# Another order of calls in an attention and feed-forward kernel on one core

## The chip, the core and the metric

The kernel runs on one core of a Trainium2 chip. The metric is the device time of one execution in microseconds (us). Before the change it is 411.36 us (median of 3 runs, 410.83 to 411.58).

## The reference

Attention with normalized q and k, followed by a feed-forward layer with a parametric ReLU, all in float32:

```python
# q, k, v: 8 x 12 x 448 x 64; w_in: 768 x 2048; w_out: 2048 x 768; alpha: 2048
def rmsnorm(x, g):
    return x / np.sqrt(np.mean(x * x, axis=-1, keepdims=True) + 1e-06) * g
scores = (1 / np.sqrt(64)) * rmsnorm(q, g_q) @ rmsnorm(k, g_k).transpose(0, 1, 3, 2)
attn = np.exp(scores - scores.max(-1, keepdims=True))
attn = attn / (attn.sum(-1, keepdims=True) + 1e-09)
x = (attn @ v).transpose(0, 2, 1, 3).reshape(3584, 768)
h = x @ w_in
out = (np.maximum(h, 0) + alpha * np.minimum(h, 0)) @ w_out
```

## The kernel before

The 96 heads (8 batches of 12) are worked in 24 groups of four heads, three groups to a batch. The order of all work is one text, PLAN: a list of some 1,300 calls such as `score(2,5,0)`, which a loop at the end of the kernel carries out one after the other. Each call issues its instructions to a fixed engine, and each engine works through its own instructions strictly in that order, waiting on semaphores for what the others must have done. So the order of PLAN decides what queues behind what on TensorE (PE), VectorE (DVE), ScalarE (ACT), GpSimd (POOL) and on the two queues that issue transfers, SyncE's (SP) and POOL's own.

For one group y the calls are these.

- `load_qk(y)` (SP) loads q and k as `nat`. The memory of q and k is taken over from an earlier group, so the transfer waits until that group's `scale` has been done.
- `square(y,nm)` (POOL for nearly all groups), `reduce(y,nm)` (DVE, sums of squares), `root(y)` (ACT, two small instructions for the inverse root), `scale(y,nm)` (DVE up to group 3, POOL from group 4 on) normalize q and k to float16.
- `turn(y)` or `turn_one(y,nm)` transposes them by matmuls on PE and copies them back by DVE, up to group 8; from group 9 on `flip` (DVE) and `weigh` (ACT) do this.
- `score(y,j,spare)` makes a block of scores on PE, seven to a group, in one of two PSUM tiles `sc` or, with spare, in a third, `acc`. `soft(y,j)` takes their exponential on ACT.
- `den` and `attend` sum the exponentials and multiply them with v on PE; `log` and `invert` (ACT) make the reciprocal of the sums; `times` (DVE) multiplies and writes the attention's result `xT`. A batch's first two groups go together (`0+1`), its third alone (`2`).

For one batch b, `up(b,ft)` multiplies `xT` with a block of 128 columns of w_in on PE (16 blocks). `slope` multiplies the result by alpha, `larger` (DVE) takes the larger of the two and writes `gT`. For batch 0, `begin(ft)` does the part of the first four blocks that needs groups 0 and 1 alone. `down` and, later, the `qa`, `qb`, `qc` and `quad` calls multiply `gT` with w_out; `mix_weights`, `mix_two` and `mix_rest` (POOL, mostly) make the sums that these use.

The first group has calls of its own, in parts by heads and columns (`part_square`, `part_reduce`, `part_root`, `part_scale`, `part_turn`, `part_copy`). `opening()` issues the transfers of groups 0, 1 and 2 and of the gains and alphas, then some matmuls on zeros (`spin`), and a transpose `ct` of gains and alphas, which `gains()` copies to where they are used; k's copies out of PSUM are multiplied by that gain. Further `spin` calls put matmuls on zeros, whose result nobody uses, between others. `follow(y,nm)` has POOL copy one element of what DVE's `scale` wrote: it makes POOL wait there for DVE. `load_w_in(c)`, `load_w_out(c)` and `load_v(b)` issue the transfers of weights and v from POOL's queue.

Of the kernel before, what the change touches and what calls it, by code (L numbers as in the profile page):

```python
# [43 lines left out]
up(0,1,0) begin(2) begin(3) root(4) up(0,2,0) up(0,3,1) up(0,4,0) scale(4,q) slope(0,0) soft(3,1)  # L44
larger(0,0) score(3,2,0) score(3,6,0) slope(0,1) load_qk(7) follow(2,k) larger(0,1) slope(0,4)
slope(0,2) slope(0,3) larger(0,4) up(0,5,0) larger(0,2) larger(0,3) root(5) soft(3,6) slope(0,5)
soft(3,2) larger(0,5) up(0,6,0) scale(4,k) turn(4) scale(5,q) up(0,8,0) score(4,0,0) slope(0,6)
score(4,1,1) square(6,k) larger(0,6) slope(0,8) score(3,5,0) up(0,9,0) load_w_out(1) scale(5,k)
soft(4,0) square(7,q) larger(0,8) up(0,11,0) load_qk(8) score(4,2,0) score(3,3,0) soft(3,5)
load_v(1) square(7,k) up(0,7,1) soft(4,1) slope(0,9) up(0,10,0) reduce(6,q) square(8,q) reduce(6,k)  # L50
load_w_out(2) soft(4,2) up(0,12,0) slope(0,11) larger(0,9) soft(3,3) score(3,4,0) slope(0,10)
score(4,3,0) larger(0,11) larger(0,10) slope(0,7) larger(0,7) up(0,13,0) soft(3,4) slope(0,12)
larger(0,12) turn(5) up(0,14,0) square(8,k) soft(4,3) score(4,6,0) slope(0,13) score(4,4,1) root(6)
slope(0,14) larger(0,13) up(0,15,0) scale(6,q) reduce(8,q) soft(4,4) score(5,4,0) larger(0,14)
scale(6,k) score(5,0,1) reduce(7,q) slope(0,15) larger(0,15) down(1,0,0) score(5,2,1) score(4,5,0)
soft(4,6) soft(5,0) soft(5,4) soft(5,2) score(5,1,0) soft(4,5) down(0,0,0) turn(6) load_w_out(3)
den(3+4,1) reduce(7,k) attend(3+4,0,0) score(5,5,0) score(5,6,0) soft(5,1) mix_weights(0,1) log(3+4)
invert(3+4) soft(5,5) soft(5,6) mix_weights(0,3) attend(3+4,1,0) score(6,0,1) score(5,3,0) soft(6,0)
score(6,4,0) down_end(0,0) down(2,0,0) soft(5,3) root(7) scale(7,q) load_qk(9) soft(6,4) scale(7,k)
den(5,0) attend(5,0,1) down_end(1,0) mix_weights(0,2) times(3+4,0,0) times(3+4,1,0) times(3+4,1,1)  # L60
load_qk(10) log(5) down(0,1,0) reduce(8,k) invert(5) down_end(2,0) times(5,0,1) times(5,0,0)
times(5,0,3) times(5,0,2) score(6,5,1) mix_weights(0,0) score(6,1,0) down_end(0,1) score(6,6,0)
soft(6,5) turn(7) up(1,1,1) square(9,q) down(1,1,0) root(8) reduce(9,q) soft(6,6) score(6,3,1)
score(7,0,0) slope(1,1) score(6,2,0) up(1,2,0) up(1,0,0) soft(6,1) soft(7,0) soft(6,3) square(9,k)
up(1,3,1) up(1,4,0) slope(1,2) slope(1,0) larger(1,1) down_end(1,1) reduce(9,k) root(9) larger(1,2)
# [1032 lines left out]
```

## Time and profile before

| | |
|---|---|
| median of 3 runs | 411.36 us (410.83 to 411.58) |
| the profiled execution | 410.69 us, with a span of 408.6 us from its first to its last instruction |
| PE busy | 395.3 us, 97% of the span |
| DVE, ACT, POOL busy | 268.3, 270.4 and 299.9 us |
| granted TensorE clock | 1.000 |
| DMA | 58.39 MB, 143 GB/s on average |

In the profile, `PE hT L726 <- DVE xT L709` reads: PE, about to write the tile hT by an instruction of line 726, waited for DVE's writing of xT by line 709. In the rows of the timeline the columns are the start in us, the duration in us from the first to the last of the instructions put together, the engine, the line, the operation, what is written and read, the shapes, and the number of instructions; in brackets stands the idle time before, with what ended it. PEld are PE's loads of weights, which overlap its matmuls. In the rows of busy time by stretches the columns are the stretch, its length, the busy us with the number of instructions for PE, PEld, DVE, ACT and POOL, the granted clock, the share of the DMA engines and GB/s.

### The profile page before, as it was taken

Reading aid. Unit: us, or ns where it says so; the run is one execution under the profiler, and the core shown is the slowest. Engines: PE = TensorE matmul, PEld = TensorE weight load, DVE = VectorE, ACT = ScalarE, POOL = GpSimd, SP = SyncE. Lnnn points to the kernel's source line nnn. Section 1 sums busy time; section 2 is a strip of 40 time slices with the busy share of each in tenths; the row PEclk is TensorE's granted clock in tenths of the full one; section 3 lists DMA queues with packets and bytes.
Section 4 is the critical chain, followed back from the end, with each engine's and each line's share of the span. In section 5 each row is a group of like instructions: output and inputs, shape, how many; then the busy total and the mean of one; then the engine's idle time right before and its main releaser. Section 6 shows DMA issues by size and latency. Waiting matters only on the chain.

```text
span 408.6 us, 11992 instructions
## 1 busy us (share of the span) xinstructions
PE 395.3 (97%) x5083; PEld 210.3 (51%) x5083; DVE 268.3 (66%) x480; ACT 270.4 (66%) x405; POOL 299.9 (73%) x200
## 2 busy tenths in 40 slices
PE   7688999999999999999999999999999999999996
PEld 3344445555455445554455455555555455655664
DVE  3957874676766685779678678886668545654422
ACT  5597686757885876767886987686876874245110
POOL 7977998497796998997796995589496809600780
PEclk9999999999999999999999999999999999999999
DMA  7999699796776794579952595794516000230143
GB/s 260 242 280 227 110 265 165 173 239 177 125 180 154 173 203 108 119 172 185 232 130 83 136 240 145 147 217 102 140 38 131 21 2 22 59 79 0 39 98 98
DMA packets 37222, 58.39 MB, mean 143 GB/s; under 512 B 4769, under 2 KB 28977, under 8 KB 37169
## 3 DMA queue, kind: packets, MB, share of 16 engines
q1 hardware_dynamic: 23232, 45.43, 43.2%
q0 software_dynamic: 13536, 11.81, 19.1%
q8 instruction: 39, 0.64, 0.7%
q10 hardware_dynamic: 400, 0.39, 0.3%
q14 instruction: 15, 0.11, 0.1%
HBM read 58.40 MB, written 11.01 MB: 170 GB/s over the span
## 4 chain that ended last, share of the span: by engine, by line
PE 88%; DVE 4%; DMA 3%; POOL 3%; issue 1%; POOLq 0%; DVEq 0%
PE hT L726 25%; PE hTa L726 9%; PE sc L588 8%; PE op L792 7%; PE qx L854 5%; PE av L613 5%; PE qz L854 4%; PE qc L854 4%; PE oq L854 4%; PE qxa L854 3%; PE avb L613 2%; PE dn L613 2%; PE oqm L854 2%; DMA w_in_sb<-in_moe_w_in_dram 2%; POOL nat L376 2%; DMA arena<-in_g_k_dram 2%
## 5 line engine op out<-in xcount | busy, mean ns | idle before, releaser
L602 ACT ACTIVATE expT<-sc 128x896 f16<-128x896 f32 x168 | 146.3, 916 | 40.9 <-PE sc L588 39.2
L726 PE MATMUL hT<-xT,w_in_sb 128*128 128x448 f16 x558 | 115.9, 353 | 1.6 <-DVE xT L709 1.4
L726 PEld LDWEIGHTS <-w_in_sb 128*128 128x128 f16 x768 | 73.0, 98 | 74.5 <-issue 9.9
L423 POOL TENSOR_TENSOR qs<-nat,rr 128x896 f16<-128x896 f32 x30 | 65.7, 2221 | 26.5 <-ACT rr L417 23.4
L766 ACT ACTIVATE gT<-hT,cols 128x448 f16<-128x448 f32 x92 | 58.4, 636 | 40.0 <-PE hT L726 38.9
L772 DVE TENSOR_TENSOR gT<-hT,gT 128x448 f16<-128x448 f32 x93 | 57.3, 619 | 38.2 <-ACT gT L766 37.5
L365 POOL TENSOR_TENSOR nat<-nat 128x896 f32<-128x896 f32 x30 | 50.7, 1697 | 8.1 <-DMA nat<-in_q_dram 7.7
L588 PE MATMUL sc<-qT,kT 64*32 64x448 f16 (+1 forms) x1092 | 49.4, 355 | 4.3 <-ACT expT L602 1.7
L854 PEld LDWEIGHTS <-gT 128*128 128x128 f16 x352 | 33.4, 98 | 25.5 <-issue 4.1
L726 PE MATMUL hTa<-xT,w_in_sb 128*128 128x448 f16 x198 | 42.9, 353 | 0.0
L842 POOL TENSOR_TENSOR gs<-gT 128x1024 f16<-128x1024 f16 x4 | 8.5, 2127 | 36.7 <-DVE gT L772 36.7
L709 DVE TENSOR_TENSOR xT<-av,rden 64x448 f16<-64x448 f32 (+1 forms) x37 | 27.2, 736 | 10.7 <-ACT rden L671 4.6
L386 DVE TENSOR_REDUCE sp<-nat 128x28 f32<-128x896 f32 x30 | 32.1, 1070 | 2.1 <-POOL nat L365 2.0
L588 PEld LDWEIGHTS <-kT 64*32 64x32 f16 (+1 forms) x1092 | 16.7, 93 | 32.4 <-issue 23.0
L792 PE MATMUL op<-w_out_sb,gT 128*128 128x384 f16 x176 | 30.3, 326 | 0.2 <-DVE xT L709 0.2
L766 ACT ACTIVATE gT<-hTa,cols 128x448 f16<-128x448 f32 x33 | 21.0, 636 | 10.5 <-PE hTa L726 10.0
L772 DVE TENSOR_TENSOR gT<-hTa,gT 128x448 f16<-128x448 f32 x33 | 20.4, 618 | 10.6 <-ACT gT L766 10.2
L613 PEld LDWEIGHTS <-vt 64*32 64x32 f16 x1344 | 19.7, 92 | 12.2 <-issue 1.9
L792 PEld LDWEIGHTS <-gT 128*128 128x128 f16 x192 | 18.3, 98 | 14.5 <-issue 3.0
L613 PE MATMUL av<-expT,vt 64*32 64x448 f16 x896 | 24.3, 350 | 0.0
L850 POOL TENSOR_TENSOR gT<-gT 128x1024 f16<-128x1024 f16 x11 | 23.5, 2133 | 0.0
L854 PEld LDWEIGHTS <-arena 128*128 128x128 f16 x136 | 12.6, 98 | 10.5 <-issue 2.3
(151 smaller groups left out, 572.5 us busy)
## 6 DMA issues: line engine op xcount, KB each, us to landing
nat<-in_q_dram SPq DMA_DIRECT2D x60, 216.0 KB, 4.1
nat<-in_k_dram SPq DMA_DIRECT2D x60, 216.0 KB, 5.0
out_dram<-osb SPq DMA_DIRECT2D x107, 96.0 KB, 3.1
vt<-in_v_dram POOLq DMA_DIRECT2D x8, 672.0 KB, 7.8
w_in_sb<-in_moe_w_in_dram POOLq DMA_DIRECT2D x24, 128.0 KB, 7.3
w_out_sb<-in_moe_w_out_dram POOLq DMA_DIRECT2D x4, 768.0 KB, 8.6
nat<-in_k_dram SPq DMA_DIRECT2D x6, 448.0 KB, 7.8
nat<-in_q_dram SPq DMA_DIRECT2D x5, 448.0 KB, 6.7
```

What stands on the lines that cost most here:

```text
L365: nc.gpsimd.tensor_mul(out=sqs[y, nm], in0=t[:, :, :HD], in1=t[:, :, :HD])
L386: nc.vector.tensor_reduce(out=parts[y][:, ts("qk".index(nm), 4 * J), :1], in_=sqs[y, nm], axis=AXIS_X, op=ALU.add,)
L423: nc.gpsimd.tensor_mul(out=t.rearrange("p j d n -> p n j d"), in0=nat[y, nm][:, :, :HD].rearrange("p (n j) d -> p n j d", j=J), in1=r.unsq ...
L588: nc.tensor.matmul(out=sc[ds(64 * g + m * c, m), par, :S].rearrange("p (j c) -> p j c", j=J), lhsT=kT[ds(64 * par, 64), j, g, ts(c, m)], r ...
L602: nc.scalar.activation(out=expT[y][:, j], in_=scs[y, j][:, :, :S], func=AF.Exp, scale=QK_SCALE, bias=EXP_BIAS,)
L613: nc.tensor.matmul(out=accs[g][ds(32 * n, 32), :S], lhsT=weights(g, y, par, c, j), rhs=expT[y][ds(64 * g, 64), j, par, :], start=(j == 0), ...
L709: nc.vector.tensor_mul(out=o, in0=p, in1=q)
L726: nc.tensor.matmul(out=hT[:, :S], lhsT=w_in_sb[:, block_of(g, i), ts(ft, 128)], rhs=xT[b][:, g, i, :], start=(i == 0 and g == 0), stop=(i ...
L766: nc.scalar.activation(out=g, in_=hT[:, :S], func=AF.Copy, scale=alpha_sb[:, ft : ft + 1])
L772: nc.vector.tensor_max(out=g, in0=hT[:, :S], in1=g)
L792: nc.tensor.matmul(out=op[:, :OH], lhsT=gT[:, ft, ts(tile % J, 128)], rhs=w_out_sb[:, ft, ts(oh, OH)], start=(ft == 0), stop=(ft == NF - 1),)
L854: nc.tensor.matmul(out=bank[:, c], lhsT=g[:, ft], rhs=v[:, ft, c], start=(first and ft == 0), stop=(ft == HF - 1), skip_group_check=True,)
```

## The change

PLAN has another order. From the start to the first `up` nearly every engine's order differs, further on the order is similar but differs in many places. In the opening: the `spin` matmuls of `opening()` come down to one call `spin(17,0)`, and of the later ones `spin(2,0)` stays; the transpose of gains and alphas is a call of its own, `factors()`, behind q's transposes; the two first reductions of q change places; `square(1,k)` goes from POOL to ACT, the copies of q and of the first part of k from DVE to ACT; `square(3,k)` comes ahead of `square(3,q)`, in two halves; w_in is loaded in halves (`load_w_in(c,lo,hi)`), spread between the squares; three of the four `follow` calls are gone, and the last comes some 220 calls later. Over the whole PLAN 25 `slope` calls are marked for DVE, where 3 were; `score`, `den`, `attend` and `up` use the third PSUM tile in other places. A `slope` and a `square` are now told their engine in PLAN, and `soft`, `begin` and `up` can be called in any order of their blocks.

The diff, with PLAN up to the first `up` of batch 0:

```diff
 PLAN = """
-opening() part_square(q,0:1,0:7,act) part_square(q,1:2,0:7,act) part_reduce(q,0:1,0:7) spin(2,0)
-part_reduce(q,1:2,0:7) part_root(q,0:7) part_square(k,0:2,0:3,act) part_scale(q,0:7,7,pool)
-part_reduce(k,0:2,0:3) part_square(k,0:2,3:7,act) square(1,q) load_w_in(1) spin(1)
-part_reduce(k,0:2,3:7) part_root(k,3:7) reduce(1,q) square(1,k) part_root(k,0:3) gains()
-part_turn(q,r0-7) load_qk(3) spin(1,0) part_scale(k,0:3,3,vec) part_turn(k,r0-3)
-part_scale(k,3:7,4,vec) part_copy(q,0:7,vec) part_turn(k,r3-7) load_v(0) reduce(1,k) follow(0,k)
-square(2,q) part_copy(k,0:3,vec) part_copy(k,3:7,vec) root(1) square(2,k) score(0,0,0) soft(0,0)
-reduce(2,q,0) score(0,4,1) load_w_in(0) score(0,3,0) spin(1) reduce(2,q,1) soft(0,3) score(0,1,0)
-scale(1,k) scale(1,q) soft(0,4) score(0,2,0) soft(0,2) reduce(2,k) score(0,6,1) turn_one(1,q)
-soft(0,1) turn_one(1,k) score(1,0,1) score(1,3,0) spin(1) score(1,2,0) soft(0,6) root(2) soft(1,0)
-load_qk(4) soft(1,3) scale(2,k) scale(2,q) follow(2,q) square(3,q) square(3,k) load_w_in(2)
-soft(1,2) score(0,5,1) score(1,1,0) soft(0,5) soft(1,1) score(1,5,0) turn(2) soft(1,5) score(1,6,1)
-soft(1,6) reduce(3,q,None) score(1,4,0) score(2,0,0) soft(1,4) den(0+1,0) follow(1,k) soft(2,0)
-log(0+1) load_qk(5) score(2,1,0) spin(1) reduce(3,k,0+1) attend(0+1,1,0) score(2,6,0) score(2,4,1)
-attend(0+1,0,1) soft(2,1) root(3) score(2,3,1) invert(0+1) scale(3,q) scale(3,k) score(2,2,0)
-load_w_in(3) soft(2,4) soft(2,6) times(0+1,1,0) times(0+1,1,1) square(4,q) times(0+1,0,0) turn(3)
-score(2,5,0) square(4,k) load_qk(6) reduce(4,q,None) soft(2,3) soft(2,2) soft(2,5) den(2,0) log(2)
-reduce(4,k,None) invert(2) attend(2,0,1) score(3,0,1) square(5,q) square(5,k) times(2,0,0)
-score(3,1,0) begin(0) reduce(5,q) square(6,q) soft(3,0) begin(1) up(0,0,0) load_w_out(0) reduce(5,k)
...
+opening() part_square(q,0:1,0:7,act) part_square(q,1:2,0:7,act) part_reduce(q,1:2,0:7)
+part_reduce(q,0:1,0:7) spin(17,0) part_root(q,0:7) part_scale(q,0:7,7,pool)
+part_square(k,0:2,0:3,act) part_reduce(k,0:2,0:3) part_square(k,0:2,3:7,act) load_w_in(1,0,4)
+part_root(k,0:3) load_v(0) part_turn(q,r0-7) part_reduce(k,0:2,3:7) factors()
+part_scale(k,0:3,3,vec) part_root(k,3:7) gains() part_scale(k,3:7,4,vec) part_turn(k,r0-3)
+square(1,k,act) square(2,q,pool,2) reduce(1,k) part_copy(q,0:7,act) square(1,q,act)
+part_copy(k,0:3,act) part_turn(k,r3-7) part_copy(k,3:7,vec) score(0,6,1) reduce(2,q,0) score(0,1,0)
+reduce(1,q) score(0,4,1) load_qk(3) soft(0,6) score(0,0,0) root(1) reduce(2,q,1) scale(1,q)
+scale(1,k) score(0,5,0) square(2,k) load_w_in(2,4,8) reduce(2,k) turn_one(1,q) score(0,3,0)
+soft(0,1) square(3,k,pool,2) soft(0,0) turn_one(1,k) load_qk(4) soft(0,4) soft(0,5) score(0,2,0)
+score(1,5,0) soft(0,3) root(2) score(1,6,1) score(1,0,0) scale(2,k) spin(2,0) score(1,2,1)
+scale(2,q) load_w_in(0,0,4) square(3,q) soft(0,2) reduce(3,k,0+1) score(1,1,0) square(4,q) turn(2)
+soft(1,6) soft(1,5) soft(1,0) load_w_in(0,4,8) soft(1,2) score(1,3,0) soft(1,1) score(1,4,1)
+reduce(3,q,None) soft(1,3) soft(1,4) den(0+1,1) load_w_in(2,0,4) score(2,0,1) root(3)
+attend(0+1,0,1) reduce(4,q,None) score(2,3,0) log(0+1) score(2,4,1) soft(2,0) attend(0+1,1,0)
+score(2,1,1) invert(0+1) load_qk(5) soft(2,4) soft(2,3) square(4,k) load_qk(6) score(2,5,0)
+score(2,2,0) soft(2,1) soft(2,5) scale(3,q) score(2,6,1) scale(3,k) square(5,q) soft(2,2)
+square(5,k) times(0+1,0,0) times(0+1,1,0) soft(2,6) times(0+1,1,1) load_qk(7) turn(3)
+reduce(4,k,None) den(2,1) log(2) load_w_in(3,0,4) attend(2,0,1) reduce(5,q) root(4) invert(2)
+begin(3) scale(4,q) times(2,0,0) begin(1) begin(2) up(0,1,0) load_w_out(1) up(0,2,0) begin(0)
+up(0,0,0) reduce(5,k) score(3,1,0) slope(0,1) scale(4,k) root(5) score(3,0,0) square(6,k)
...
-    def load_w_in(c):
+    def load_w_in(c, lo, hi):
...
+        for m in range(lo, hi):
+            e, n = divmod(m % 4, 2)
...
+            if m < 4:
+                src = moe_w_in[:512].rearrange("(n x p) f -> n p x f", n=4, p=32)
...
+            else:
+                src = moe_w_in[512:].rearrange("(n g e p) f -> e n p g f", n=2, g=2, e=2)
...
-    def square(y, nm):
+    def square(y, nm, eng=None, n=1):
...
+            if eng is nc.scalar:
+                nc.scalar.activation(out=sqf[:, c], in_=src[:, c], func=AF.Square)
...
-        if nm == "k":
+        if nm == "k" and eng is nc.scalar:
+            nc.scalar.activation(out=o, in_=tp, func=AF.Copy, scale=gain[:, 0:1])
+        elif nm == "k":
...
     def soft(y, j):
-        if j == 0:
+        if y not in expT:
...
-        elif ft == 2:
+        elif ft not in begun:
...
                 up_part(begun[n], 0, n, G - 1, G)
+                raised[0, n] = begun[n], gT[:, n, :S]
...
-    def slope(b, ft):
+    def slope(b, ft, eng=None):
         hT, g = raised[b, ft]
-        if b == 0 and ft in (2, 3, NF - 4):
+        if eng is nc.vector:
...
         load_qk(1, True)
         load_qk(2)
 
-        spin(2)
-        spin(17, False)
+    def factors():
         ct = psf.tile([128, 512], FP32, name="ct", tag="mm")
         nc.tensor.transpose(ct[:, : NF + 2], rows, ident32[: NF + 2, : NF + 2])
```

More of the change, by code (lines that the diff above doesn't have):

```diff
@@ L43 @@
-score(3,1,0) begin(0) reduce(5,q) square(6,q) soft(3,0) begin(1) up(0,0,0) load_w_out(0) reduce(5,k)
[L44 to L65, printed above, removed]
@@ new lines @@
+square(8,k) larger(0,9) reduce(8,k) larger(0,10) score(4,6,1) root(6) reduce(7,k) down(1,0,0)
+score(5,5,1) score(4,2,0) score(4,4,0) soft(4,6) square(8,q) soft(5,2) down(0,0,0) score(5,6,0)
+reduce(7,q) reduce(8,q) scale(6,k) score(5,3,0) soft(4,4) follow(0,k) scale(6,q) root(7) load_qk(9)
+soft(4,2) turn(6) down_end(0,0) scale(7,q) den(3+4,1) attend(3+4,0,1) load_qk(10) soft(5,5)
+soft(5,6) attend(3+4,1,0) down_end(1,0) soft(5,3) den(5,1) log(3+4) invert(3+4) attend(5,0,1)
+scale(7,k) score(6,0,1) log(5) score(6,4,0) times(3+4,0,0) down(2,0,0) mix_weights(0,2) down(0,1,0)
@@ new lines @@
+score(6,5,1) invert(5) times(3+4,1,0) times(3+4,1,1) times(5,0,0) times(5,0,1) load_v(2)
+times(5,0,3) down_end(2,0) square(9,q) times(5,0,2) score(6,6,0) score(6,1,0) square(9,k)
+reduce(9,q) soft(6,0) soft(6,4) root(8) down_end(0,1) turn(7) up(1,1,1) up(1,0,0) slope(1,0,vec)
+down(1,1,0) score(6,2,0) score(6,3,1) larger(1,0) mix_weights(0,1) up(1,4,0) soft(6,5) up(1,3,0)
+score(7,4,1) soft(6,6) mix_weights(0,0) score(7,0,0) load_qk(11) slope(1,1) larger(1,1) score(7,2,0)
+up(1,7,0) scale(8,q) soft(6,1) down_end(1,1) reduce(9,k) up(1,2,0) soft(6,2) soft(6,3) load_qk(12)
@@ new lines @@
+larger(1,12) reduce(10,q) up(1,13,0) score(8,0,0) square(11,q) mix_weights(1,3) score(8,3,0)
+slope(1,11) larger(1,11) soft(7,3) den(6+7,0) down(2,1,0) slope(1,14) fold(10) root(10) scale(10,k)
+flip(9,q) square(11,k) slope(1,15) flip(9,k) slope(1,13) larger(1,14) load_qk(13) score(8,1,0)
+soft(8,3) score(8,5,1) larger(1,15) score(8,4,0) larger(1,13) down(3,0,0) scale(10,q) log(6+7)
+score(8,6,0) invert(6+7) soft(8,0) soft(8,1) reduce(11,q) down_end(2,1) reduce(11,k) down_end(3,0)
+flip(10,k) soft(8,5) score(8,2,0) soft(8,4) weigh(9) attend(6+7,0,0) attend(6+7,1,0) fold(11)
@@ L1034 @@
     acts = dict(
+        factors=factors,
         attend=attend, begin=begin, den=den, den_pre=den_pre, down=down, down_end=down_end,
```

278 lines of the change are left out of this document (137 added, 141 removed).

## The prediction

> **What bounds the kernel now.** I read four views in this order: the page's shares and slices, the busy time in two stretches, TensorE's own waits, and the timeline of the first 45 us, where the change lies. The profiled execution took 410.69 us with a span of 408.6, so 2.1 lie outside the span; the median of the runs shown is 411.36, 0.67 above this execution. I sum against 410.69 and add 0.67 at the end. 0.2% of this kernel, about what a measurement can tell from no change, is 0.8 us.
>
> ```profile
> PE   7688999999999999999999999999999999999996
> 0.00:41.30 41.30, 32.55 (x470) 15.78 (x471) 27.58 (x42) 29.26 (x47) 33.69 (x53) 1.00 1.02 250
> 41.30:408.60 367.30, 362.71 (x4614) 194.50 (x4613) 240.71 (x439) 241.11 (x358) 266.25 (x148) 1.00 0.59 131
> PE hT L726 <- DVE xT L709: 0.2, 1, 0.2
> PE sc L588 <- DVE kT L569: 0.2, 1, 0.2
> PE op L792 <- DVE xT L709: 0.2, 1, 0.2
> ```
>
> The slices show TensorE (PE) full from the fifth on. From 41.3 us it is busy 362.71 of 367.30 us, and its listed waits there are three of 0.2 us; what else is missing lies behind its last matmul. So from 41.3 us the end is set by the amount of PE work. Before 41.3 PE is also marked busy for 32.55 us, but much of that is `spin` and matmuls whose successors wait. What the change can win is how early PE becomes full. These rows end the opening:
>
> ```profile
> 32.59 0.56 POOL L339 DMA_DIRECT2D w_in_sb<-in_moe_w_in_dram  x1 [1.10 <-DMA w_in_sb<-in_moe_w_in_dram]
> 34.08 1.71 POOL L339 DMA_DIRECT2D w_in_sb<-in_moe_w_in_dram  x3 [0.93 <-DMA w_in_sb<-in_moe_w_in_dram]
> 35.80 3.33 POOL L376 TENSOR_TENSOR nat<-nat 128x896 f32<-128x896 f32 x2
> 39.16 1.09 DVE L395 TENSOR_REDUCE ss<-nat 128x14 f32<-128x896 f32 x1 [0.55 <-POOL nat L376]
> 40.16 1.08 DVE L709 TENSOR_TENSOR xT<-av,rden 128x896 f16<-128x896 f32 x1
> 41.30 0.92 PE L726 MATMUL hT<-xT,w_in_sb 128*128 128x448 f16 x4 [1.23 <-DVE xT L709]
> ```
>
> Read upward: up(0,0) waits 1.23 us for xT of group 2 (times(2,0,0), VectorE, DVE). That stood behind reduce(4,k), which waited 0.55 for GpSimd's (POOL) square(4,k). POOL was late because it had issued w_in(2) and w_in(3) first, waiting 1.10 and 0.93 for earlier transfers.
>
> **The change, step by step.** I walk the new order through these rows, shifting times by what precedes each call.
>
> ```profile
> 3.92 1.15 DVE L457 TENSOR_REDUCE ss<-nat 128x7 f32<-128x448 f32 x2 [2.51 <-ACT nat L450]
> 5.65 1.69 POOL L474 TENSOR_TENSOR qs<-nat,rr 128x896 f16<-128x896 f32 x1 [1.34 <-ACT rr L469]
> 7.29 2.25 POOL L339 DMA_DIRECT2D w_in_sb<-in_moe_w_in_dram  x4
> 10.65 0.62 DVE L1030 TENSOR_TENSOR gain<-cols 128x1 f32<-128x1 f32 x1
> 11.15 0.91 POOL L329 DMA_DIRECT2D vt<-in_v_dram  x1
> 11.19 1.15 DVE L474 TENSOR_TENSOR qs<-nat,rr 128x384 f16<-128x384 f32 x2
> 12.55 3.46 POOL L376 TENSOR_TENSOR arena<-arena 128x448 f32<-128x448 f32 x3
> 12.79 1.07 DVE L395 TENSOR_REDUCE ss<-nat 128x14 f32<-128x896 f32 x1
> 13.79 0.79 DVE L495 TENSOR_SCALAR kT<-tps,gain 128x384 f16<-128x384 f16 x2
> 13.90 0.23 ACT L416 ACTIVATE rr<-ss 128x28 f32<-128x28 f32 x1 [3.94 <-DVE ss L395]
> 14.68 4.97 ACT L602 ACTIVATE expT<-sc 128x896 f16<-128x896 f32 x6 [0.30 <-PE sc L588]
> 15.55 2.41 DVE L436 TENSOR_TENSOR arena<-nat,rr 128x896 f16<-128x896 f32 x2
> 20.13 2.08 DVE L436 TENSOR_TENSOR qs<-arena,rr 128x896 f16<-128x896 f32 x2
> ```
>
> *First scores.* The two q reductions (1.15 together) swap, so the first must wait for the second square: 0.55 later for part_root(q). POOL's part_scale(q) then runs from 6.20 to 7.89, four w_in issues (2.25) to 10.1, load_v (0.91) to 11.05, and there square(2,q) starts, since follow(0,k), which held it to 12.55, is now far later. `gains` still ends at 11.27, because it waits for a transfer that no edit moves, and part_scale(k,3:7) is ready at 11.19, 0.14 us into POOL's half square (3.46 for two halves and a whole: 0.9 a half). Do they collide? The pair of scale(1) calls, of which the first began while POOL's square ran on to 16.01, took 2.41 us; the same pair for group 2, with no square beside it, took 2.08. So an overlap of 0.46 (15.55 to 16.01) cost 0.33, two thirds of it; by that share the overlap of 0.8 with the half square would cost 0.55. The bounds are nothing and 1.7 (both halves first). I take 0.8, the first half waited out to its end, because the row also fits a wait for all but the last of the square.
>
> The Trainium skill, "SBUF — State Buffer", section "Who interferes with whom", has a rule that speaks against dropping the follow() calls: a DVE tensor_tensor with both inputs in SBUF and a GpSimd op that reads SBUF share one read port, and the second to issue waits the whole other instruction out. By that rule the cost is 0.8 and by the row's share 0.55, which would make the sum 0.25 lower; the 2.41 against 2.08 agrees with it in kind.
>
> So part_scale(k,3:7) ends at 12.6, reduce(1,k) (1.07) at 13.7, the vector copy of k (half of 0.79) at 14.05, and the first exponential on ScalarE (ACT) some 0.5 later, as before (copy 13.79 to 14.2, exponential 14.68): at 14.5, only 0.2 sooner. The copy of q, the copy of k's first part and both squares of group 1 lie on ACT from about 9.4 on, where it stood idle for 3.94 us ahead of root(1) at 13.90; no row shows ACT copying transposes from PSUM; at the 0.83 of an exponential from there (4.97 for six) four such steps fill 3.3 of that stretch, and even at 1.2 each they end at 14.2, in time: I put nothing. Beyond that, each excess would go straight to the first exponential; a gain is excluded, since k waits for `gains` and not for ACT.
>
> *ACT from 14.5 on.* It has 21 exponentials, three roots, log and invert before the last exponential of group 2.
>
> ```profile
> 20.24 7.50 ACT L602 ACTIVATE expT<-sc 128x896 f16<-128x896 f32 x9 [0.23 <-PE sc L588]
> 27.77 0.92 ACT L666 ACTIVATE rden<-dn 128x896 f32<-128x896 f32 x1
> 27.96 1.02 PE L1000 MATMUL spin<-gT 128*128 128x448 f32 x2
> 35.08 0.92 ACT L602 ACTIVATE expT<-sc 128x896 f16<-128x896 f32 x1 [0.48 <-PE sc L588]
> 35.13 0.67 DVE L569 TENSOR_SCALAR kT<-tps,gain 128x896 f16<-128x896 f16 x1
> 36.74 0.92 ACT L666 ACTIVATE rden<-dn 128x896 f32<-128x896 f32 x1 [0.74 <-PE dn L613]
> 37.69 0.95 ACT L671 ACTIVATE rden<-rden 128x896 f32<-128x896 f32 x1
> 36.42 1.52 PE L613 MATMUL av<-expT,vt 64*32 64x448 f16 x56
> 37.87 0.57 PE L588 MATMUL sc<-qT,kT 64*64 64x448 f16 x8
> 38.37 1.69 PE L726 MATMUL hT<-xT,w_in_sb 128*128 128x448 f16 x8
> ```
>
> Nine exponentials in 7.50 are 0.83 each: 17.5 for 21. A root is two instructions of 0.23 (13.90's row is a first) and a little, 1.45 for three; log and invert (0.92 and 0.95, each overlapping its neighbour a little) 1.7. Root(1) now stands behind the first exponential and waits for reduce(1,q), which comes after part of reduce(2,q): 14.05 + 0.54 + 1.07 = 15.66 against 15.42, a wait of 0.25, for which 0.1 more is put for scores that follow one another closely. Sum: 14.5 + 21.0 = 35.5 for the end of the last exponential, against 36.0 (35.08 + 0.92). The wait of 0.48 in front of the last exponential goes because its score no longer stands behind turn(3), and the `spin` of 1.02 at 27.96 no longer stands in front of the first attend.
>
> *From the last exponential to xT.* The log follows it by 0.74 as before: 36.25 to 37.15; root(4) now stands between (0.45), then invert (0.95) to 38.55. The multiply times(2,0,0) must not find DVE occupied: turn(3) ended at 35.8 before (35.13 + 0.67) and comes no later now, and reduce(4,k) and reduce(5,q) (1.09 each) end at 38.0. Their squares: POOL has square(3,k) once k of group 3 has landed, about 19 (an estimate: half the DMA time to 41.3 stands ahead of it, at a share of 1.02 all through), 20.8; four w_in issues (0.56 each), 23.0; square(3,q) and square(4,q) (1.67 each, half of 3.33), 26.4; eight issues, 30.9; square(4,k), square(5,q), square(5,k), 35.9. Square(5,q) is there at 34.2 and would hold times(2,0,0) only from 37.4 on: a cover of 3.2 us. Times(2,0,0) runs from 38.6 to 39.65, where it ended at 41.24 before.
>
> *PE.* Den(2) ends at 36.1, attend(2) (1.45 to its successor) at 37.55, three begin() (0.75 each, from the 8 matmuls in 38.37's row, 0.19 apart) at 39.8, past 39.65: no wait for xT. But by 41.30 the old order had also done score(3,0), score(3,1) (0.5) and two begin() (1.5). So 37.55 + 2.0 = 39.55 corresponds to 41.30: **1.75 us won**.
>
> *The rest.* All later PE work is the same; counting both orders from there, PE turns 56 times from matmuls over the full array to scores or attention and 56 times back in each, and which bank a score uses costs PE nothing unless it waits. The w_in halves are the same transfers. Of the slopes, 22 more move from ACT to DVE: beside PE, unless DVE fills up (below). I put nothing for them. Sum: 410.69 - 1.75 = 408.9 profiled, **409.6** as median.
>
> **The rivals.**
>
> *A, no collision at the port.* POOL starts square(2,q) after part_scale(k). For it: half a transfer issue shifts it. Then 0.8 earlier from the first score on: 408.8.
>
> *B, a transfer decides.* DMA is full up to 41 us (share 1.02), and in-order POOL now puts square(3,k) ahead of w_in(0). If a landing holds POOL by more than the 3.2 us of cover, times(2,0,0) is again behind reduce(5,q); at 5 us late nothing is won: 411.4. Against it: w_in comes in halves, so half of w_in(0) no longer stands ahead of q and k of group 4.
>
> *C, the granted TensorE clock falls: slower.* All but two of the `spin` groups go.
>
> ```profile
> 1.47 3.35 PE L1000 MATMUL spin<-gT 128*128 128x448 f32 x4 [1.47 <-DVE gT L262]
> 6.49 0.15 PEld L1000 LDWEIGHTS <-ident 128*128 128x128 f16 x1 [0.22 <-issue]
> 6.86 1.82 PEld L1000 LDWEIGHTS <-ident 128*128 128x128 f16 x10 [0.22 <-issue]
> ```
>
> The first spins are 0.37 us apart, those from 6.86 on 0.18 (ten in 1.82): PE starts at half speed and has the full one some 5.4 us after its first matmul. Afterwards the old order never leaves it idle for long. In the new one I count, between 8.4 and 13.9, only 14 transposes and one small matmul, with gaps up to 1.9 us. If it falls, den(0+1), the two attends and the scores between 27 and 32.5 (5.4 us until it is back) take twice as long: the end of den 0.45, an attend 1.5 (36.42's row) and three scores (0.57 a pair) 0.85, in all 2.8, on ACT's path since its scores stand behind them: 409.6 + 2.8 = 412.4. It decides from the point where a stretch of idling lets the clock drop; this trace has none. The Trainium skill, "TensorE: Matmul & The Clock Gate", section "What's actually happening", puts that at a whole idle window of some 3.4 us, which the gaps here would not reach; no run here shows such a window.
>
> *D, DVE becomes the bound in batch 1's up().*
>
> ```profile
> 85.40:110.50 25.10, 25.10 (x181) 12.35 (x186) 18.45 (x35) 19.68 (x32) 19.51 (x13) 1.00 0.83 181
> L761 DVE TENSOR_SCALAR gT<-hTb,cols 128x448 f16<-128x448 f32 x2 | 1.3, 679 | 0.0
> ```
>
> DVE is busy 18.45 of 25.10 us there; six slopes at 0.68 make 22.5. It decides if it has 2.6 us more; if all six reached PE, they would cost 4.1: 413.7. ACT (19.68) gets lighter by as much, which speaks for it as a trade that goes unseen.
>
> **How the numbers follow.** The forecast 0.56 (408.9 to 410.4 by the uncertain 0.8 of the collision and the landing), A 0.13, B 0.11, C 0.12, D 0.08. Faster by over 0.8 us means below 410.5: 0.52 of the forecast, A, and 0.04 of the others: 0.69. Within 0.8: the rest of the forecast, B nearly whole, a part of C: 0.17. Slower: most of C and D: 0.14. The range takes A with some PE waits fewer (408.1) and B with a little of C (411.8), leaving out D and C's end.
>
> **What would show it.** Right: first exponential near 14.5; part_scale(k,3:7) over 1 us long or starting late beside square(2,q); last exponential of group 2 near 35.5; times(2,0,0) at 38.6 without DVE held by a reduce; PE full from about 36 with begin() before up(0,1); w_in issues without waits near 1 us. Wrong: matmuls 0.37 apart after 8 us (C); POOL's square(5,q) ending past 37 us (B); PE waits for gT between 85 and 110 us (D).

## The result, and the profile after

The changed kernel takes **422.27 us** (median of 4 runs, 420.43 to 423.48) against 411.36 before: ratio 1.0264, 95% interval 1.0222 to 1.0305. Forecast were 409.6 and a range up to 411.8: wrong in sign and size. Medians are over all runs; ratios here and below leave out runs over 1.5% above the kernel's fastest (two of e4, one each of e8 and e11, three of e17). The profiled execution took 422.94 us (span 420.7), 12.25 above that of before. In the 40 slices (tenths busy) one dent shows, the 7 in the eighth slice, 73.6 to 84.1 us; TensorE's waits from 45 us on (engine, line and what was waited for, then sum, times, longest) show more:

```profile
PE   6669999799999999999999999999999999999996
PEclk9568999899999999999999999999999999999999
```

```profile
PE avb L616 <- issue: 2.9, 1, 2.9
PE sc L591 <- DVE xT L712: 0.8, 1, 0.8
PE sc L591 <- DVE osb L930: 0.4, 1, 0.4
PE sc L591 <- ACT expT L605: 0.4, 1, 0.4
...
```

Before, three waits of 0.2 us stood here. Now one of 2.9 has no releaser ("issue"), and some of 0.4 to 0.8 name VectorE and ScalarE. Line numbers are 1 to 6 higher than before (L437 is the old L436, L616 the old L613). First the opening, in the timelines of VectorE, GpSimd and TensorE (start, duration, what, idle time before it and its releaser):

```profile
20.25 7.32 DVE L437 TENSOR_TENSOR qs<-arena,rr 128x896 f16<-128x896 f32 x2
...
19.31 1.82 POOL L377 TENSOR_TENSOR nat<-nat 128x448 f32<-128x448 f32 x2 [2.52 <-DVE ss L396]
21.08 2.21 POOL L345 DMA_DIRECT2D w_in_sb<-in_moe_w_in_dram  x4
23.30 3.32 POOL L377 TENSOR_TENSOR nat<-nat 128x896 f32<-128x896 f32 x2
...
27.64 1.68 PE L563 MATMUL tps<-ident,qs 128*128 128x128 f16 x14 [3.87 <-DVE qs L437]
...
42.50 0.93 PE L729 MATMUL hTb<-xT,w_in_sb 128*128 128x448 f16 x4
...
43.52 1.09 DVE L712 TENSOR_TENSOR xT<-av,rden 128x896 f16<-128x896 f32 x1 [0.97 <-ACT rden L674]
```

The two scale(2) calls, 2.08 before, take 7.32 together: scale(2,k) 20.25 to 22.08, scale(2,q) 22.00 to 27.58, which is 0.96 behind the end of GpSimd's second whole square (23.30 + 3.32 = 26.62). Turn(2) waits 3.87 for it, and the first begin() starts at 42.50 where 37.55 was forecast. By the prediction's count (two scores and two begin() more done by 41.30, 2.0 us) 42.50 is 3.2 *behind* the old order, not 1.75 ahead. The other 9.0 us are lost later. The largest piece, in TensorE's timeline and the clock by windows (us, five engines' busy time and counts, granted clock, DMA share, GB/s):

```profile
76.26 1.52 PE L616 MATMUL av<-expT,vt 64*32 64x448 f16 x56
77.58 1.51 PE L616 MATMUL avb<-expT,vt 64*32 64x448 f16 x52
81.99 0.56 PE L616 MATMUL avb<-expT,vt 64*32 64x448 f16 x4 [2.89 <-issue]
```

```profile
6.60:10.01 3.41, 1.32 (x11) 0.59 (x9) 1.67 (x3) 2.41 (x7) 3.41 (x5) 1.00 1.02 353
10.01:13.42 3.41, 1.32 (x8) 0.91 (x8) 2.07 (x5) 2.53 (x4) 3.41 (x5) 0.50 1.05 241
...
16.83:20.25 3.42, 3.18 (x26) 1.59 (x22) 3.35 (x6) 3.39 (x7) 0.94 (x2) 0.50 1.21 230
20.25:23.66 3.41, 3.19 (x22) 0.93 (x22) 3.41 (x3) 3.02 (x4) 3.40 (x6) 0.50 1.10 293
23.66:27.08 3.42, 0.11 (x4) 0.00 (x0) 3.42 (x1) 1.90 (x3) 3.42 (x3) 1.00 1.08 213
...
78.28:81.69 3.41, 0.81 (x36) 0.25 (x13) 1.09 (x1) 0.14 (x1) 0.00 (x0) 1.00 0.99 249
81.69:85.10 3.41, 3.11 (x96) 2.27 (x104) 1.16 (x2) 1.12 (x2) 0.00 (x0) 0.50 1.02 241
85.10:88.50 3.40, 3.40 (x50) 1.72 (x35) 1.87 (x3) 2.07 (x5) 2.31 (x2) 1.00 1.03 226
```

Attend(3+4,1) does 52 of its 56 matmuls, stands for 2.89 us with no releaser, and does the last 4; in the next window the clock is at half. The transfer engines are full (0.99). Another count sets the time from one TensorE call to the next against the usual time of the same pair of calls (an estimate). By it the old trace loses 3 us from 41 us to the end and the new one 12: 4.9 of them between 70 and 90 us, some 6 in about twenty waits of 0.2 to 0.8 behind 100 us (old: 1.7).

### The profile page after: what moved, and what is told of

Read it like the earlier page. It is cut to its first block, busy times and chain, and to the rows that moved or that the text cites. A ratio compares the mean times of both kernels' runs of the same rounds, so it can differ in the third digit from the quotient of the medians.

```text
span 420.7 us, 11959 instructions
## 1 busy us (share of the span) xinstructions
PE 398.8 (95%) x5070; PEld 211.4 (50%) x5070; DVE 287.6 (68%) x500; ACT 260.2 (62%) x386; POOL 297.9 (71%) x196
## 3 DMA queue, kind: packets, MB, share of 16 engines
HBM read 58.40 MB, written 11.01 MB: 165 GB/s over the span
## 5 line engine op out<-in xcount | busy, mean ns | idle before, releaser
L770 ACT ACTIVATE gT<-hT,cols 128x448 f16<-128x448 f32 x73 | 46.1, 633 | 35.9 <-PE hT L729 35.4
L591 PE MATMUL sc<-qT,kT 64*32 64x448 f16 (+1 forms) x1092 | 52.0, 366 | 4.6 <-ACT expT L605 1.9
L729 PE MATMUL hTa<-xT,w_in_sb 128*128 128x448 f16 x204 | 44.2, 353 | 0.2 <-DVE kT L572 0.2
L770 ACT ACTIVATE gT<-hTa,cols 128x448 f16<-128x448 f32 x30 | 19.1, 635 | 23.5 <-PE hTa L729 23.3
L616 PEld LDWEIGHTS <-vt 64*32 64x32 f16 x1344 | 20.2, 94 | 15.6 <-issue 5.9
L616 PE MATMUL av<-expT,vt 64*32 64x448 f16 x896 | 25.6, 360 | 0.0
```

Of the source, the lines that this page charges most:

```text
L591: nc.tensor.matmul(out=sc[ds(64 * g + m * c, m), par, :S].rearrange("p (j c) -> p j c", j=J), lhsT=kT[ds(64 * par, 64), j, g, ts(c, m)], r ...
L616: nc.tensor.matmul(out=accs[g][ds(32 * n, 32), :S], lhsT=weights(g, y, par, c, j), rhs=expT[y][ds(64 * g, 64), j, par, :], start=(j == 0), ...
L729: nc.tensor.matmul(out=hT[:, :S], lhsT=w_in_sb[:, block_of(g, i), ts(ft, 128)], rhs=xT[b][:, g, i, :], start=(i == 0 and g == 0), stop=(i ...
L770: nc.scalar.activation(out=g, in_=hT[:, :S], func=AF.Copy, scale=alpha_sb[:, ft : ft + 1])
```

## The experiments

Theories at the start. For the opening's 3.2 us, *lock-out*: VectorE cannot go on while GpSimd's squares run, because follow(2,q) went. Or *clock*: it is the half clock, because the spin calls went. For the later 9 us, *supply*: TensorE runs out of instructions, which come as transfers; *slopes*: VectorE is overfull (rival D of the prediction); *late opening*: it only follows from the first loss.

"Opening" below is the start of the first begin() in the profiled execution (39.3 would be level with the old kernel); "later" is what that execution lost against before's 410.69 beyond its opening, by the count of 2.0 us above (with the old opening, by the start of up(0,0,0): 41.30 before, 43.30 in e3, 42.29 in e14). Ratios are to the old kernel on the same chip. In e15 and e16 (1.82) a half of square(3,k), which stands ahead of the follow call, ran on into scale(2,q).

| run | median, us | ratio, 95% interval | scale(2,q) | opening | later |
|---|---|---|---|---|---|
| changed | 422.27 | 1.0264 (1.0222 to 1.0305) | 5.58 | 42.50 | 9.0 |
| e1_follow | 420.83 | 1.0242 (1.0155 to 1.0329) | 1.08 | 38.91 | 9.4 |
| e2_spins | 424.47 | 1.0306 (1.0241 to 1.0370) | 5.58 | 42.77 | 10.2 |
| e3_old_opening | 426.48 | 1.0349 (1.0274 to 1.0424) | 1.09 | old | 15.5 |
| e4_old_rest | 414.46 (10 runs, 410.72 to 419.16) | 1.0021 (0.9973 to 1.0069) | 1.08 | 37.56 | 2.3 |
| e5_spread | 420.22 | 1.0229 (1.0180 to 1.0278) | 1.08 | 36.80 | 10.2 |
| e6_late_loads | 424.40 | 1.0309 (1.0272 to 1.0346) | 1.08 | 36.87 | 15.7 |
| e8_slopes | 436.90 | 1.0578 (1.0516 to 1.0639) | 5.58 | 41.93 | 21.0 |
| e9_mixed | **409.62** (7 runs, 409.04 to 410.03) | **0.9941** (0.9919 to 0.9964) | 1.09 | 37.89 | 0.4 |
| e10_late_loads2 | 420.73 | 1.0208 (1.0181 to 1.0234) | 1.09 | 37.11 | 12.2 |
| e11_old_no_follow | 412.81 (10 runs, 410.86 to 418.9) | 1.0013 (0.9988 to 1.0037) | 1.08 | old | |
| e12_old_no_spins | 411.14 | 0.9980 (0.9961 to 1.0000) | 1.08 | old | |
| e13_bank | 420.12 (one run) | | 1.08 | 37.85 | 10.9 |
| e14_old_early_load | 415.92 | 1.0086 (1.0055 to 1.0118) | 1.08 | old | 4.4 |
| e15_later_load | 420.12 | 1.0198 (1.0155 to 1.0242) | 1.82 | 37.80 | 10.1 |
| e16_log_first | 422.14 (one run) | | 1.82 | 38.11 | 12.6 |
| e17_mixed_no_follow | 411.24 (12 runs, 408.19 to 416.83) | 0.9954 (0.9925 to 0.9984) | 1.08 | 36.76 | 0.9 |
| e18_times_first | 421.78 (one run) | | 1.08 | 37.42 | 13.0 |

### Which half of the order loses the time: e3, e4

```
e3: calls up to and with up(0,0,0) as in the old plan, all later ones as in the new plan
e4: calls up to and with up(0,0,0) as in the new plan, all later ones as in the old plan
```

> The old kernel's order of calls up to and with up(0,0,0), the changed kernel's order for all calls after it. As the prediction had it (the later order costs nothing): 411.4 within 1 us. Theory 'supply' (TensorE runs out of instructions at 78.7 us because den(3+4), two attend, den(5) and attend(5), 560 matmuls and weight loads, now follow one another while the transfers are full): the wait stays, 414 to 420. Theory 'late opening' (the later losses are only a consequence of the transfers that the late opening bunched up): gone, 411 to 412.

> The changed kernel's order up to and with up(0,0,0), the old kernel's order for the calls after it (without its spin and follow calls of the opening; score(3,0) in the other bank). If the later loss of 8.9 us belongs to the later order: only the opening's 3.3 us are left, 414.5 to 415.5. If it comes out of the late opening: 420 to 423.

The later order is the loss: with the old opening it costs 426.48, above every expectation and more than the changed kernel. The new opening with the old rest is level with the old kernel by the ratio, though its runs scatter over 8.4 us. "Late opening" falls. And the opening of e4's profiled run is the forecast one; its VectorE and TensorE rows:

```profile
20.37 2.08 DVE L437 TENSOR_TENSOR qs<-arena,rr 128x896 f16<-128x896 f32 x2
...
38.56 1.09 DVE L712 TENSOR_TENSOR xT<-av,rden 128x896 f16<-128x896 f32 x1 [1.26 <-ACT rden L674]
...
37.56 0.93 PE L729 MATMUL hTb<-xT,w_in_sb 128*128 128x448 f16 x4
...
44.79 1.29 PE L729 MATMUL hT<-xT,w_in_sb 128*128 128x448 f16 x6 [2.01 <-DVE gT L776]
```

Both scale(2) in 2.08, begin() at 37.56 (forecast 37.55), times(2,0,0) 38.56 to 39.65 (forecast 38.6 to 39.65): 1.74 won. It is lost again at 44.79: up(0,4) waits 2.01 for VectorE's first larger(), that of up(0,0), which this order had put last of the first blocks.

### The opening: e1, e2, e12, e9, e17, e11

```diff
 e1 (changed kernel)   +follow(2,q) ahead of square(3,q)
 e2 (changed kernel)   +spin(8,0) +spin(4,0) +spin(2,0) +spin(2,0) +spin(3) in TensorE's gaps
 e12 (old kernel)      -spin(2,0) -spin(1) -spin(1,0) -spin(1) -spin(1) -spin(1)
```

> The changed kernel with one call put back: follow(2,q) ahead of square(3,q), so that GpSimd cannot start that square before scale(2,q) is over. Theory 'lock-out' (the opening's loss comes from scale(2,q) on VectorE standing out GpSimd's squares, 5.58 us instead of 1.08): scale(2,q) takes 1.1 to 1.3 us, turn(2) starts near 24 instead of 27.64, the wait of 3.9 us on TensorE ahead of it goes below 1, and the time falls by 3 to 5 us, to 417 to 419. Rival 'clock' (the loss comes from the clock at half in the opening, the spins being gone): scale(2,q) may get shorter, but the scores and den(0+1) still run at half clock, den(2) and times(2,0,0) end within 1 us of where they end now, 421 to 422.

> The changed kernel with spin matmuls in TensorE's idle stretches of the opening and nothing else: spin(8,0) after part_turn(q), spin(4,0) before part_turn(k,3-7), spin(2,0) after each of two scores of group 0, spin(3) before turn(2). Theory 'clock': the granted clock is 1.0 from 6.6 us on, scores take 0.38 and den(0+1) 1.5, and most of the opening's 3.3 us comes back: 418.5 to 419.5. Rival 'lock-out': scale(2,q) still lasts till 27.6, turn(2) still waits for it, and only what follows it at half clock gets shorter (den(0+1) 2.84 to 1.56, the scores by 0.2 each): 1 to 2 us, 420.3 to 421.3.

> The old kernel without its six spin calls after the opening() group (2+1 matmuls on the identity, 8 wide ones). Theory 'clock' (half speed in the opening costs time in itself): the granted clock falls to 0.5 somewhere between 10 and 30 us and the time rises by 1 to 3 us, 412.5 to 414.5. Rival (the opening is bound by ScalarE and VectorE, TensorE has room): the clock falls, but scores only use up waits, 410.5 to 412.

With the one call back (e1), scale(2,q) takes 1.08 again, turn(2) starts at 24.51 and the opening is 3.6 us sooner; the profiled execution gains 3.2 of the 3 to 5 expected, the median 1.4 within wide intervals. In e2 scale(2,q) still lasts to 28.62, as the lock-out has it, but the run says little more on the clock: the spins took a PSUM bank, `factors()` waited 1.49 us for ScalarE's copy, and 424.47 is above what either theory expected. e12 is the clean test. The clock falls (0.53 in the mean of 16 us) and the time does not rise:

```profile
13.40:29.50 16.10, 13.25 (x148) 6.09 (x148) 12.40 (x18) 13.34 (x20) 13.73 (x21) 0.53 1.15 254
```

So the half clock costs nothing measurable in the old opening. No cost shows in the new one either: e4's opening came at the forecast time with the clock at half from 10.17 to 23.82.

```diff
 e9   new opening, +follow(2,q) ahead of square(3,q), then
      begin(0) begin(1) begin(3) up(0,0) begin(2) up(0,1) up(0,2), then nearly the
      old order, without its follow(2,k)
 e17 (e9)           -follow(2,q)
 e11 (old kernel)   -follow(2,q)
```

> The changed kernel's opening with follow(2,q) ahead of square(3,q), then begin(0), begin(1), begin(3), up(0,0), begin(2), up(0,1), up(0,2) and the old kernel's order for the rest. If the opening's gain (1.75 us as predicted, 1.67 in the profile of the kernel with the old rest) is real and the later order was the loss: 409.3 to 410.5. If follow(2,q) or the later landing of group 3 eats it: 411 to 412.5. If the loss follows the opening anyway: above 414.

> The kernel of e9_mixed (409.62, seven runs within 409.0 to 410.0) without its one call follow(2,q). Theory 'lock-out by order of issue': a race between the landing of q(3) and scale(2,q); in some runs VectorE is held up for 4 to 5 us, so the runs scatter between 409 and 415 and the median is 410 to 413. Rival (the port costs nothing here): 409 to 410, no wider than with the call.

> The old kernel with follow(2,q) left out and nothing else. Theory 'lock-out by order of issue' (GpSimd holds the port from the moment its sequencer lets square(3,q) through, also while that square still stands behind transfer issues): here w_in(0)'s eight issues end at 21.15 and q(3) has landed by then, while scale(2,q) begins at 21.13 to 21.2, so it is nearly a tie. Where GpSimd is first, scale(2,q) ends only behind square(3,q) and the two halves of square(3,k), 4 to 5 us later than 22.2, and the kernel takes 413 to 416. Where VectorE is first, square(3,q) waits 1 us, scale(2,q) takes 1.08, and it is 410.5 to 412. Rival 'follow() does nothing': scale(2,q) 1.08 and no wait on either side, 411.4.

e9 is **faster than both kernels**, 409.62, though by only 0.6% of the old one (the interval lies wholly under 1), and its seven runs lie within 1 us. Its GpSimd and TensorE rows:

```profile
20.12 2.21 POOL L345 DMA_DIRECT2D w_in_sb<-in_moe_w_in_dram  x4
22.49 0.19 POOL L510 COPY mark<-qs 128x1 f16<-128x1 f16 x1 [0.16 <-DVE qs L437]
22.63 1.68 POOL L377 TENSOR_TENSOR nat<-nat 128x896 f32<-128x896 f32 x1
...
40.17 0.54 PE L729 MATMUL hT<-xT,w_in_sb 128*128 128x448 f16 x2
```

Follow(2,q) (22.49) waits 0.16, the square comes behind scale(2,q), and up(0,0) starts at 40.17 instead of 41.30. Without that one call (e17) the best run is 0.9 us faster, and the runs scatter over 8.6 us, where the old kernel's 18 on the same chip scatter over 3.2. That is what a race would give; but e17's one trace is of a run that VectorE won, so no trace shows what held its slower runs.

What decides the race can be looked for in the traces' semaphore records. In all three traces with 5.58 us, GpSimd's sequencer let square(3,q) through *before* scale(2,q) began: 21.14 against 22.00 (changed), 22.17 against 23.04 (e2), 21.59 against 22.13 (e8). In e4, e5, e6 and e17, all without the call and with 1.08, it was after: 21.43 against 21.37, 21.31 against 21.22, 22.20 against 21.45, 22.15 against 21.92. In the first three the square itself starts some 2 us after its release, behind transfer issues: in the changed kernel at 23.30. VectorE had 1.30 us from 22.00 to there, more than the 1.08 it needs, so it was shut out before the square ran. In e11 the two came within 0.06 us, the release first (21.95 against 22.01), and there scale(2,q) still took 1.08 and square(3,q) 2.11. So release ahead of begin fits seven traces of eight and not the near tie; no run set it at will. e11's ratio shows no change; five of its runs lie above 412.8, but only one trace was taken.

### Instruction supply: e14, e6, e10, e15, e5

A wait with no releaser could be many things. Its place tells. The changed kernel stands ahead of its 859th matmul, and so do e1, e8, e13, e16 and e18 (e3 and e14, with the old opening, ahead of the 858th and 857th); e2, with 22 more matmuls ahead, stands in the same attend() 22 matmuls sooner, at the 859th of its own count:

```profile
77.85 0.94 PE L616 MATMUL avb<-expT,vt 64*32 64x448 f16 x30
82.11 1.67 PE L616 MATMUL avb<-expT,vt 64*32 64x448 f16 x26 [3.32 <-issue]
```

In e1, e8 and e18 a second wait stands ahead of the 987th (e3: the 986th): 128 matmuls and 128 weight loads on. Each time a 16 KB packet of the queue of kind "instruction" lands 1.2 to 1.7 us before TensorE goes on (changed: it starts at 79.05, lands at 80.38, matmul at 81.99). e14 makes the condition in the old kernel, by one load:

```diff
 e14 (old kernel)
-... attend(3+4,1,0) ... load_qk(9) ...
+load_qk(9) den(3+4,1) attend(3+4,0,0) ... attend(3+4,1,0) ...
```

> The old kernel with one call moved: load_qk(9) (8 transfers of 216 KB) ahead of den(3+4) instead of behind attend(3+4,1), so some 5 us sooner. Theory 'supply': the packets of instructions for the attention calls between 70 and 82 us now queue behind these transfers, as in the new order; a wait of 1 to 3 us with no releaser appears on TensorE at an edge 128 matmuls from the last one, and the time rises to 412 to 414.5. If the queue does not matter: 411 to 412 and no such wait.

Expected 412 to 414.5, measured 415.92 (the old kernel on this chip: 412.42), with a wait of the expected kind and size. First e14, TensorE's timeline and windows, then the old kernel's:

```profile
75.13 1.31 PE L616 MATMUL avb<-expT,vt 64*32 64x448 f16 x41
79.15 0.94 PE L616 MATMUL avb<-expT,vt 64*32 64x448 f16 x15 [2.71 <-issue]
```

```profile
70.00:75.00 5.00, 5.00 (x141) 2.94 (x138) 3.14 (x5) 2.17 (x3) 2.41 (x2) 1.00 1.09 222
...
80.00:85.00 5.00, 5.00 (x75) 2.50 (x76) 2.50 (x4) 2.87 (x5) 2.17 (x2) 0.76 0.31 72
```

```profile
74.13 1.52 PE L613 MATMUL avb<-expT,vt 64*32 64x448 f16 x56
75.58 0.76 PE L588 MATMUL sc<-qT,kT 64*64 64x448 f16 x12
```

```profile
70.00:75.00 5.00, 5.00 (x175) 2.87 (x179) 3.90 (x6) 2.67 (x4) 2.15 (x2) 1.00 0.73 117
...
80.00:85.00 5.00, 5.00 (x91) 2.68 (x76) 3.05 (x5) 1.78 (x3) 5.00 (x4) 1.00 1.04 249
```

The old attend(3+4,1) runs through in 1.52; with the loads ahead of it (DMA share 1.09 instead of 0.73) it stands 2.71 us after 41 matmuls, and the clock is at half for a while behind (0.76). The packet shows the delay too: the sixth of its queue starts when 1,526 matmuls and weight loads have begun in the old kernel, in e14 only at 1,713, where TensorE stops. The old kernel's traffic is as dense at 80 to 85 us, but from 81.2 on TensorE does down() there, 16 matmuls in 2.7 us, and no wait shows; an attend() uses up 112 instructions in 1.5 us. As far as these traces go it takes both, dense instructions and full transfers.

```diff
 e6 (changed)   load_qk(9), load_qk(10) behind down_end(2,0)
 e10 (e1)       the same, and reduce(9,q) behind down_end(1,1)
 e15 (e1)       load_qk(9), load_qk(10) behind down_end(1,0)
 e5 (changed)   down(0,0,0) between the two attend(3+4), down(2,0,0) ahead of den(5)
```

> The changed kernel with load_qk(9) and load_qk(10) (16 transfers of 216 KB) issued behind down_end(2,0), after the attention calls of batch 0, instead of ahead of them. Theory 'supply through full transfer queues': the packet of instructions is fetched at once, the wait at the 859th matmul is below 0.5 us, 417 to 418.5. Rival 'supply, whatever the transfers' (128 matmuls of 13 ns issue are more than the fetch can bring in any case): the wait stays at 3 us, 421 to 423. Group 9 is needed only from 118 us on, so its later arrival should cost nothing under either.

> The changed kernel with follow(2,q) back (as in e1_follow, 420.83) and load_qk(9), load_qk(10) issued behind down_end(2,0); this time reduce(9,q) stands behind down_end(1,1), so that VectorE doesn't wait for the later group 9 ahead of turn(7). Theory 'supply through full transfer queues': no wait at the 859th matmul or at the 987th, TensorE at full clock from 34 us on, 415 to 417 (12.4 us of losses after the opening in e1_follow, of them 5 between 73 and 86 us). If the later loads only move the wait (group 9 or 10 late on GpSimd): 419 to 421.

> The changed kernel with follow(2,q) back (420.83 before) and load_qk(9), load_qk(10) issued behind down_end(1,0), some 4 us later than there but 8 us sooner than in e10_late_loads2. Theory 'supply': the wait at the 859th matmul shrinks from 3.3 us to under 1, the one at the 987th may be 1 to 1.5; if group 9 is then in time for VectorE and GpSimd, 416 to 418.5. If what is won is given back at up(1,...) as in e10_late_loads2: 419.5 to 421.

> The changed kernel with two calls of 16 matmuls each moved among the attention calls of batch 0: down(0,0,0) to between the two attend(3+4), down(2,0,0) to between attend(3+4,1) and den(5). TensorE has the same work; only the count of instructions per microsecond falls there. Theory 'supply' (at the 859th matmul TensorE stands until the next 256 instructions have come through the full transfer queues): the 128 matmuls before that edge take 6.2 us instead of 3.6, the wait of 3.1 us goes to about 0.5, the half-speed window after it goes too, and the time falls by 4 to 5 us, to 417.5 to 418.5. Rival 'data' (the wait is for something that attend(3+4,1) or den(5) needs): it stays where the call stands, 421 to 423.

With the loads out of the way the wait at that place is gone in all three (e6, e10, e15); e6's TensorE:

```profile
70.62 1.52 PE L616 MATMUL av<-expT,vt 64*32 64x448 f16 x56
71.95 1.52 PE L616 MATMUL avb<-expT,vt 64*32 64x448 f16 x56
73.27 0.87 PE L640 MATMUL dn<-expT,ones 64*32 64x224 f16 x56
...
91.58 0.91 PE L563 MATMUL tps<-ident,qs 128*128 128x128 f16 x7 [8.84 <-DVE osb L807]
```

Five attention calls in a row, no gap; packets start at 70.48 and 74.14. But no time is won: turn(7) stands 8.84 us, since VectorE's queue has reduce(9,q) ahead of what releases its bank, and group 9 now lands late. In e10 TensorE waits 5.2 us at up(1,7) for VectorE instead, in e15 3.4 at turn(7). My expectation that group 9 had until 118 us overlooked that a reduce or a square blocks its engine in order. In e5, with matmul work between the attention calls, the wait without a releaser shrinks from 3.1 (e1) to 0.2, but others came, TensorE's from 60 to 85 us:

```profile
PE sc L591 <- ACT expT L605: 1.8, 2, 1.0
PE op L796 <- DVE xT L712: 0.7, 1, 0.7
PE avb L616 <- DVE osb L807: 0.6, 1, 0.6
...
PE avb L616 <- issue: 0.2, 1, 0.2
```

Two are for banks that the moved down() calls need sooner; the first is ScalarE, behind which TensorE, 2.1 us sooner than in e1, now runs.

So supply is shown as the cause of the wait. But no run of the later order won its 9 us back: where the wait went, others came, and in the table a sooner opening mostly goes with a larger later loss.

### The small waits: e8, e13, e16, e18

```diff
 e8 (changed)  20 of the 22 slope(..,vec) back to ScalarE
 e13 (e1)      -score(10,0,1) +score(10,0,0)
 e16 (e1)      log_pre(8) ahead of soft(9,3) soft(9,5)
 e18 (e1)      reduce(12,q) fold(12) behind all times(8,..), flip(10,q) behind three of them
```

> The changed kernel with 20 of the 22 slopes that went to VectorE put back on ScalarE, in the same order. Theory 'VectorE load' (the prediction's rival D, and the some 4 us of small waits after 110 us): these waits go, 2 to 4 us, 418 to 420. Rival (the small waits come of where the calls stand in TensorE's order): within 1 us of the changed kernel, 421.5 to 423; where ScalarE is now the fuller engine it may be slower by 1 to 2.

> The changed kernel with follow(2,q) back (as in e1_follow) and score(10,0) in the other PSUM pool (as the old order had it). Theory 'banks' (the small waits of the later order are matmuls whose PSUM bank VectorE has not emptied): the 0.84 us lost between down(4,1) and score(10,0) near 138 us go and nothing else in the later order changes by over 0.2. Rival 'data' (group 10's q or k is late): it stays.

> The changed kernel with follow(2,q) back and log_pre(8) ahead of soft(9,3) and soft(9,5) on ScalarE, as the old order had it. Theory 'order of calls on ScalarE' (the wait of 0.84 us between down(4,1) and score(10,0), which moved to up(2,0) when the bank was changed, is for times(8,...), late behind two exponentials of 0.9): the wait goes or is below 0.2, and no other of the later small waits changes by more than 0.2 except near it. If it is VectorE's or GpSimd's load: it stays.

> The changed kernel with follow(2,q) back and, on VectorE, times(8,...) ahead of reduce(12,q) and fold(12), which stood in front of them. Theory 'order of calls on VectorE' (the 0.84 us between down(4,1) and score(10,0) are VectorE's queue: five calls between den_pre(8) and times(8,0,3)): the loss there falls below 0.2 us, as in the old order, and the kernel's other small losses stay. Rival 'TensorE simply runs closer behind': the wait moves to another call within 5 us and the sum over that stretch stays over 0.8.

With the slopes back on ScalarE the later order loses 12 us more, which neither expectation allowed for, at places like these (TensorE's waits of e8 from 100 us):

```profile
PE hT L729 <- DVE gT L776: 3.4, 4, 1.6
PE hTa L729 <- ACT expT L605: 2.7, 2, 2.3
...
```

So rival D had the sign wrong: in this order the move to VectorE is a gain. Of the waits left I followed the largest, 0.8 us ahead of score(10,0). The other bank (e13) moved it to up(2,0); ScalarE's order (e16) left it, and 0.9 at a score came, behind an exponential. VectorE's order (e18) took it away there, and 0.9 at up(2,0), 0.8 at up(2,7) and 1.4 at down(5,0) came, all three behind VectorE. These three are single runs. It seems to hang on VectorE's queue as a whole, not on one call; some 4 us of such waits are not settled further.

## Why the prediction was wrong, step by step

- **What bounds the kernel.** Read rightly for the opening: with VectorE not shut out, everything from scale(2) to the first begin() came as forecast (e4). The sentence that failed is "from 41.3 us the end is set by the amount of PE work": the profile showed TensorE full *in that order*; it did not say that another order keeps it full.
- **First scores.** Square(2,q) started at 11.01 (forecast 11.05), the first exponential at 14.46 (14.5), by luck: two misses cancel. The collision priced at 0.8 fell the other way: `gains` ended at 10.73, where 11.27 was forecast, and part_scale(k,3:7), now 0.68, went first. The four ACT steps, put at nothing, held the k transposes 1.52 us:

```profile
12.59 0.58 PE L486 MATMUL tps<-ident,qs 128*128 128x128 f16 x4 [1.52 <-ACT kT L496]
```

- **The port.** Mechanism right, place and size wrong. I walked the removal of follow(0,k) through the rows and priced it; follow(2,q) I passed by, though in the old trace it waits 1.19 us for VectorE and three squares follow, which says what it holds back:

```profile
22.34 0.19 POOL L507 COPY mark<-qs 128x1 f16<-128x1 f16 x1 [1.19 <-DVE qs L436]
22.48 3.46 POOL L376 TENSOR_TENSOR nat<-nat 128x896 f32<-128x896 f32 x3
```

In the new order two whole squares stood ready there: 4.5 us (5.58 less 1.08) instead of 0.8. The pair scale(3) met later squares in the same way: 4.01 us in the changed kernel, 2.08 in e1. The Trainium skill, "SBUF — State Buffer", section "Who interferes with whom", says that order of issue decides who blocks. If the sequencer's release counts as issue, seven of the eight traces above agree, and e11 does not.

- **Last exponential 35.5, xT 38.6 to 39.65, 1.75 won.** 35.55, 38.56 to 39.65 and 1.74 in e4; 40.81 and 43.52 to 44.61 in the changed kernel.
- **"The rest", put at nothing: 9.0 us.** The term that decided. Counting mode turns checked one cost of an order and left three: how many instructions a stretch uses while transfers are full (2.89 us here, 2.4 to 5.0 over the runs; e14 shows it by 3.5 us in the median), the half clock behind such a stop, and in-order waits on VectorE and ScalarE. By the count above, the stretch of the first two loses 4.9 us; of the small waits it is not shown which call causes them.
- **Rival C.** The clock did fall, from 10.01 on, though no window was wholly idle; its price of 2.8 was wrong for the opening: no cost in e12, and none seen in e4. The Trainium skill, "TensorE: Matmul & The Clock Gate", section "What's actually happening", speaks of an idle window; here a window with 1.32 of 3.41 us busy was enough.
- **The range** held no case in which the later order itself costs time, and ended at 411.8.

## What to carry over

Before a new order of calls is costed, list for every in-order guard that it drops (a wait, a marker, a spin) what stands ready behind it, and price each place alone; an order that one trace shows need not hold in the next run where nothing enforces it. "The bound engine is full" holds for the order that was profiled: with a new one, look at what it must be fed, and count the instructions per microsecond in dense stretches against what the transfers leave free. When a small wait is moved, see whether the sum falls before calling it mended.
